# Attention, forward and backward in one stream: two constant matmuls between the score rows of three half-steps in four, the backward part two half-steps later, and the normalisation cut in two

## The chip, the cores and the metric

The kernel runs on one core of one Trainium2 chip. The metric is device time in microseconds (us) of one execution, as the median of several runs. A second execution is recorded by the profiler; its own time and the span of its instructions are given below beside the median. The engines are called PE (TensorE, the matrix unit), ACT (ScalarE), DVE (VectorE), POOL (GpSimd) and SP (SyncE, which issues the DMAs).

## What is computed

The reference mixes two branches of a layer and returns the output together with the gradients of all its weights. The branch that matters here is multi-head attention over 2048 tokens with 32 heads of width 18:

```
qkv = (x @ wqkv) -> q, k, v           # 32 heads, width 18
scores = q k^T * 18 ** -0.5
p = softmax(scores);  o = p v;  a = o @ wo
out = g * a + (1 - g) * b             # b: a state-space convolution
grads = vjp(out)(grad_out)            # of x, wqkv, wo and ten others
```

The backward pass of attention needs, for each head and each pair of token blocks, the probabilities once with keys along the partitions and once with queries along them, the product of dO with V, `ds = p * (dO V^T - delta)`, and three contractions that give dV, dQ and dK.

## The kernel before, in words

The kernel has five stages. The first projects q, k and v (up to about 240 us). The second is the attention stage, from about 240 to 2533 us; the change is in it alone. After it come the output projections and weight gradients, the convolution branch and its gradients, and a final mixing stage.

**Tiling.** Four heads form a group `g` (8 groups); each head is padded to 32 partitions, so that four heads fill 128. Queries are taken in blocks `b` of 512 (4 blocks), so there are 32 units `(g, b)`. Keys are taken in 16 tiles `i` of 128.

**The loop.** The stage is written out by hand: `manual_schedule` fixes the order of instructions on PE, ACT, DVE and POOL as the program emits them. The order on SP is left to a planner. The loop variable is a half-step `G`; 32 of them (`NST`) are a unit, 1024 in all (`NTOT`). The forward work of half-step `G` and the backward work of half-step `G2 = G - OFF` are interleaved; `OFF` is 37 before the change, so the backward stream of a unit starts when the forward stream is five half-steps into the next one. `s` below is the number of a half-step in its unit.

**One half-step.** In two rounds `x = 0, 1`, PE computes three *rows* each, a matmul of 32 partitions by 512 columns on a quarter of the array. P1 makes a block of forward scores; ACT turns it into `PT` (L592). P3 makes the same scores with queries along the partitions; ACT turns it into `eb` (L596). P2 is dO V^T; DVE multiplies it by `PT` into `ds` (L601). Rows of P1 and P3 share four PSUM banks ("S"), rows of P2 two ("dP"). So ACT has four exponentials a half-step and DVE two products.

**Bursts.** After the rows come the contractions, with 32 output partitions each so that four run side by side on quarters of the array: eight matmuls of 512 columns for dV (`dv_burst`), eight for dQ (`dq_burst`), twice eight of 256 columns for dK (`dk_half`), in this order over four half-steps that will be called phases 0 to 3 (`G2 % 4`). They share one PSUM bank, `accB`. At the end of phases 0, 1 and 3 DVE adds the bank to a sum in SBUF (`ev`: L461 `dvacc`, L478 `dqa`, L502 `dkacc`). The forward contraction `accO` has a bank of its own and four matmuls in two of the four half-steps (`G % 4` of 3 and 0). Before the change these are phases 2 and 3.

**Normalisation.** When `accO` of a unit is complete, `post_forward` copies it out on ACT (`f0`). Two half-steps later (`s` = 2) `f1` transposes it on PE into an "S" bank and has six DVE instructions (L397 to L407): the reciprocal, `Ob`, `dOa`, their product, its sum, and minus that sum as an extra column of `dOa`. Then two DMAs are issued, one storing `Ob` and (`f2`) one transposing `dOa` into `dOaT`, which the rows P2 of the backward stream read.

**Group loads.** Every four units the operands of the next group are loaded. The tiles `VaT`, `Ktok` and `Qtok` exist once, so their loads wait for the last reader of the group before.

Of the kernel before, what the change touches and what calls it, by code (L numbers as in the profile page):

```python
# [12 lines left out]
F32 = mybir.dt.float32  # L13
# [4 lines left out]
P = 128  # L18


def build(tc, aps, dbg_aps=None, stages=("s1", "attn", "post", "s4", "final")):
# [39 lines left out]
    with ExitStack() as gctx:  # L61
# [280 lines left out]
        if "attn" in stages:  # L342
            KB = 512
            NQ = S // KB
            TPQ = KB // P
            DA = HP
            with ExitStack() as ctx:
                ctx.enter_context(tc.manual_schedule(engines={mybir.EngineType.PE, mybir.EngineType.Activation, mybir.EngineType.DVE, mybir.EngineType.Pool}))
                ga = ctx.enter_context(tc.tile_pool(name="ga", bufs=2))
                ptp = ctx.enter_context(tc.tile_pool(name="ptp", bufs=20))  # L350
                work = ctx.enter_context(tc.tile_pool(name="awork", bufs=2))
                apsp = ctx.enter_context(tc.tile_pool(name="aps", bufs=1, space=bass.MemoryType.PSUM))
                ident_f = work.tile([P, P], F32, tag="ident_f", bufs=1, name="ident_f")
# [30 lines left out]
                def post_forward(g, b, acc):  # L384
                    U = UN[(g, b)]
                    st = {}

                    def f0():
                        st["oT"] = work.tile([P, KB], F32, tag="oT", name="oT")
                        nc.scalar.copy(st["oT"], acc)  # L390

                    def f1():
                        po = apsp.tile([P, TPQ, 4, HP], F32, tag="S", bufs=4, name="ps_o")
                        for qi in range(TPQ):
                            nc.tensor.transpose(po[:, qi, :, :].rearrange("p a b -> p (a b)"), st["oT"][:, qi * P:(qi + 1) * P], ident_f)
                        rl = work.tile([P, TPQ, 4], F32, tag="rl", name="rl")
                        nc.vector.reciprocal(rl, po[:, :, :, DH])  # L397
                        rlb = rl.unsqueeze(3).to_broadcast([P, TPQ, 4, DH])
                        Ob = work.tile([P, TPQ, 4, DH], BF, tag="Ob", name="Ob")
                        da = U["dOa"]  # L400
                        nc.vector.tensor_tensor(Ob, po[:, :, :, 0:DH], rlb, op=A.mult)
                        nc.vector.tensor_tensor(da[:, :, :, 0:DH], U["dO"], rlb, op=A.mult)
                        prod = work.tile([P, TPQ, 4, DH], F32, tag="prod", bufs=1, name="prod")
                        nc.vector.tensor_tensor(prod, da[:, :, :, 0:DH], Ob, op=A.mult)
                        dl = work.tile([P, TPQ, 4], F32, tag="dl", name="dl")
                        nc.vector.tensor_reduce(dl, prod, axis=AX.X, op=A.add)
                        nc.vector.tensor_scalar(da[:, :, :, DH], dl, -1.0, None, op0=A.mult)  # L407
                        nc.sync.dma_start(O_d[:, b * TPQ:(b + 1) * TPQ, 4 * g * DH:4 * (g + 1) * DH], Ob.rearrange("p t a b -> p t (a b)"))

                    def f2():  # L410
                        U["dOaT"] = work.tile([P, TPQ, P], BF, tag="dOaT", name="dOaT")
                        nc.sync.dma_start_transpose(out=U["dOaT"], in_=U["dOa"].rearrange("p t a b -> p (t a b)"))
                    return f0, f1, f2
# [18 lines left out]

                NST = 2 * NT
                NU = NG * NQ
                OFF = NST + 5
                units = [(g, b) for g in range(NG) for b in range(NQ)]
                accO = {}
                todo = {}
# [1 line left out]
                def at(n, f):  # L440
                    todo.setdefault(n, []).append(f)

                def accB(name):
                    return apsp.tile([P, KB], F32, tag="accB", name=name)

                def dv_burst(g, b, kq, half):
                    U = UN[(g, b)]
                    acc = accB("accV")
                    for n_ in range(2):
                        ii = 2 * half + n_  # L450
                        for j in range(4):
                            mm(acc[HP * j:HP * (j + 1), :], lhsT=U["dOa"][:, ii, j, :], rhs=U["eb"].pop((kq, ii, j)),
                               start=(n_ == 0), stop=(n_ == 1), tile_position=(0, HP * j))

                    def ev():
                        if b == 0 and half == 0:
                            DKV[("v", g, kq)] = work.tile([P, KB], F32, tag="dvacc", bufs=4, name="dvacc")
                            nc.vector.tensor_copy(DKV[("v", g, kq)], acc)
                        else:
                            a_ = DKV[("v", g, kq)]  # L460
                            nc.vector.tensor_tensor(a_, a_, acc, op=A.add)  # L461
                    return ev

                def dq_burst(g, b, p):
                    U = UN[(g, b)]
                    acc = accB("accQ")
                    for n_ in range(2):
                        i = 2 * p + n_
                        for j in range(4):
                            mm(acc[HP * j:HP * (j + 1), :], lhsT=grp_t[g]["Ktok"][:, i, j, :], rhs=U["ds"][i][:, j, :],  # L470
                               start=(n_ == 0), stop=(n_ == 1), tile_position=(0, HP * j))

                    def ev():
                        if p == 0:
                            U["dqa"] = work.tile([P, KB], F32, tag="dqa", name="dqa")
                            nc.vector.tensor_copy(U["dqa"], acc)
                        else:
                            nc.vector.tensor_tensor(U["dqa"], U["dqa"], acc, op=A.add)  # L478
                    return ev

                def dk_half(g, b, p, h, st):
                    U = UN[(g, b)]
                    if h == 0:
                        st["acc"] = accB("accK")
# [22 lines left out]
                for G in range(NTOT + OFF + 16):  # L507
# [13 lines left out]
                    if 0 <= G2 < NTOT:  # L521
                        u2, s2 = divmod(G2, NST)
                        r2 = (units[u2][0], units[u2][1], s2)
                    rows = []
                    for x in range(2):
                        if r1:
                            g, b, i, j0 = r1
                            T = grp_t[g]
                            rows.append(("P1", g, b, i, j0 + x, row("P1", g, b, T["KaT"][:, i * P:(i + 1) * P], T["QaT"][:, b * KB:(b + 1) * KB], j0 + x)))
# [10 lines left out]
                            j2 = 2 * par_ + (1 - x)  # L540
                            rows.append(("P2", g, b, i2, j2, row("P2", g, b, T["VaT"][:, i2 * P:(i2 + 1) * P], U["dOaT"].rearrange("p t q -> p (t q)"), j2)))
                    evs = []
                    if G % 4 == 1 and G2 >= 4:
                        p_ = (G2 - 4) // 4
                        if p_ < NTOT // 4:
                            u_, q_ = divmod(p_, NST // 4)
# [4 lines left out]
                    if G % 4 == 2 and G2 >= 5:  # L551
# [7 lines left out]
                    if G % 4 in (3, 0) and G2 >= 10:  # L559
                        p_ = (G2 - 10) // 4  # L560
                        if p_ < NTOT // 4:
                            u_, q_ = divmod(p_, NST // 4)
                            g, b = units[u_]
                            h_ = 0 if G % 4 == 3 else 1
# [7 lines left out]
                    if G % 4 in (3, 0) and G >= 3:  # L572
                        i_ = (G - 3) // 4 * 2 + (1 if G % 4 == 0 else 0)
                        u_, i_ = divmod(i_, NT)
                        if u_ < NU:
# [6 lines left out]
                            if i_ == NT - 1:  # L582
                                f0, f1, f2 = post_forward(g, b, accO.pop((g, b)))
                                evs.append(f0)
                                at(("pre", G + 2), f1)
                                at(("pre", G + 2), f2)
                    for (kind, g, b, i, j, ps) in rows:
                        U = UN[(g, b)]
                        if kind == "P1":
# [735 lines left out]
```

## Time and profile before

| what | value |
|---|---|
| median of 2 runs | 3977.11 us (3976.38 to 3977.84) |
| profiled execution, its own time | 3971.29 us |
| span of its instructions | 3969.6 us |
| mean granted PE clock | 0.624 of full speed |
| busy share of the span: PE, DVE, ACT | 77%, 74%, 73% |
| attention stage, first to last `PT` | 241.7 to 2467.5 us |
| its last part, backward work alone | 2467.5 to 2533.2 us |

The page of the profile gives busy time by engine, a strip of 40 slices (each 99 us) with the busy tenths of each engine and the PE clock in tenths, the chain of work that ended last, and the costliest groups of instructions with the idle time in front of them. A busy PE record runs from a matmul's issue to its modelled end, and matmuls overlap, so a PE that is always busy need not be at its peak. In the names of matmuls the moving operand stands first: `ps_P<-QaT_g,KaT_g` is a row P1, `ps_P<-KaT_g,QaT_g` a row P3, `ps_P<-dOaT,VaT_g` a row P2.

### The profile page before, as it was taken

What the parts mean: (1) busy time and instruction counts of PE and PEld (TensorE: products, weight loads), DVE (VectorE), ACT (ScalarE), POOL (GpSimd) and SP (SyncE); (2) the same over time, 40 slices, a digit from 0 to 9 for tenths busy, and PEclk for the clock granted to TensorE, in tenths of its full rate; (3) what the DMA queues carried; (4) which work ended last, traced back from release to release, by engine and by line L of the source; (5) the groups of instructions that cost most, each with busy time, mean ns of one, the idle gap of its engine ahead of it and who ended that gap; (6) DMA issues with size and microseconds to landing.
All of it is one profiled execution on the core that took longest, in us unless ns stands there. A gap on an engine that the chain in (4) does not pass through costs nothing. (4 is left out here: it accounts for less than half of the span.)

```text
span 3969.6 us, 64388 instructions
## 1 busy us (share of the span) xinstructions
PE 3044.3 (77%) x24050; PEld 1070.9 (27%) x24050; DVE 2943.6 (74%) x5147; ACT 2878.8 (73%) x5308; POOL 62.9 (2%) x141
## 2 busy tenths in 40 slices
PE   8979999999999999999999999598255444544411
PEld 2312222222222222222222222145133333333310
DVE  5628878878778778878778788521488888888877
ACT  4569999989989989989999998311466666666401
POOL 0000000000000000000000000100000000000000
PEclk9956656656566556666665565599565555555555
DMA  8537787887787887887887887966455655665457
GB/s 196 168 98 129 136 160 131 136 160 130 137 158 132 135 158 133 140 157 132 148 150 127 141 142 127 226 173 140 80 104 108 112 104 104 108 109 99 72 145 175
DMA packets 1858940, 538.18 MB, mean 136 GB/s; under 512 B 1771744, under 2 KB 1837354, under 8 KB 1858627
## 3 DMA queue, kind: packets, MB, share of 16 engines
q1 hardware_dynamic: 1858626, 534.07, 70.5%
q8 instruction: 189, 3.10, 0.3%
q14 instruction: 125, 1.02, 0.1%
HBM read 102.10 MB, written 60.96 MB: 41 GB/s over the span
## 5 line engine op out<-in xcount | busy, mean ns | idle before, releaser
L601 DVE TENSOR_TENSOR ds<-ps_P,PT 128x512 bf16<-128x512 f32 x2048 | 1355.2, 687 | 359.7 <-PE ps_P L30 235.5
L592 ACT ACTIVATE PT<-ps_P 128x512 bf16<-128x512 f32 x2048 | 1303.5, 641 | 146.8 <-PE ps_P L30 134.2
L596 ACT ACTIVATE eb<-ps_P 128x512 bf16<-128x512 f32 x2048 | 1318.8, 646 | 21.3 <-PE ps_P L30 21.2
L30 PE MATMUL ps_P<-dOaT,VaT_g 32*128 32x512 bf16 x2048 | 1072.5, 550 | 40.8 <-DMA VaT_g<-VaT_d 31.8
L30 PE MATMUL ps_P<-KaT_g,QaT_g 32*128 32x512 bf16 x2048 | 1030.5, 541 | 34.6 <-ACT PT L592 6.1
L30 PE MATMUL ps_P<-QaT_g,KaT_g 32*128 32x512 bf16 x2048 | 978.3, 556 | 30.0 <-DMA KaT_g<-KaT_d 6.0
L30 PEld LDWEIGHTS <-KaT_g 32*128 32x128 bf16 x2048 | 145.8, 101 | 672.5 <-issue 655.8
L30 PE MATMUL accO<-PT,Vtok_g 128*32 128x512 bf16 x2048 | 307.9, 585 | 0.0
L30 PEld LDWEIGHTS <-VaT_g 32*128 32x128 bf16 x2048 | 192.2, 96 | 409.2 <-issue 368.6
L30 PE MATMUL accK<-dsT,Qtok_g 128*32 128x256 bf16 x4096 | 293.2, 381 | 10.7 <-DMA Qtok_g<-QaT_d 5.4
L30 PE MATMUL accQ<-ds,Ktok_g 128*32 128x512 bf16 x2048 | 242.6, 568 | 1.3 <-DVE dvacc L461 0.8
L30 PE MATMUL accV<-eb,dOa 128*32 128x512 bf16 x2048 | 242.0, 567 | 0.6 <-DVE dkacc L502 0.6
L30 PEld LDWEIGHTS <-QaT_g 32*128 32x128 bf16 x2048 | 174.0, 98 | 168.5 <-issue 157.0
L30 PE MATMUL uvp<-RX,E1e 128*128 128x64 bf16 x1152 | 134.2, 290 | 106.3 <-DVE E1e L892 106.3
L30 PE MATMUL tps<-RX,T0w 128*128 128x32 bf16 x576 | 38.4, 233 | 215.2 <-DVE yd L1027 189.9
L873 ACT ACTIVATE kk<-ph,magc 128x512 f32<-128x512 f32 x144 | 91.2, 686 | 147.7 <-DVE E1e L891 112.7
L30 PE MATMUL ph<-thr,lrow 3*128 3x512 bf16 x288 | 126.7, 569 | 86.8 <-ACT ab L866 60.1
L461 DVE TENSOR_TENSOR dvacc<-dvacc,accV 128x512 f32<-128x512 f32 x224 | 153.5, 685 | 34.5 <-PE accV L30 31.0
L478 DVE TENSOR_TENSOR dqa<-dqa,accQ 128x512 f32<-128x512 f32 x224 | 153.2, 684 | 26.6 <-PE accQ L30 22.6
L30 PEld LDWEIGHTS <-E1e 128*128 128x128 bf16 x1152 | 125.3, 123 | 127.3 <-DVE E1e L892 126.7
L30 PE MATMUL ybp<-Rw,E1n 128*128 128x31 bf16 x1152 | 70.1, 233 | 103.5 <-ACT ydi L964 100.8
L878 DVE SCALAR_TENSOR_TENSOR kk<-kk,ph 128x512 f32<-128x512 f32 x144 | 95.1, 681 | 73.0 <-ACT kk L873 73.0
(273 smaller groups left out, 3374.9 us busy)
## 6 DMA issues: line engine op xcount, KB each, us to landing
T0w<-Kp_d SPq DMA_DIRECT2D x36, 512.0 KB
dsT<-ds SPq DMA_TRANSPOSE x512
dqkv_d<-dtk SPq DMA_DIRECT2D x96, 72.0 KB
dqkv_tok<-dqkv_d SPq DMA_DIRECT2D x1, 6912.0 KB
Md_d<-mst SPq DMA_DIRECT2D x144, 36.0 KB
ga_d<-ga_st SPq DMA_DIRECT2D x16, 288.0 KB
dxm_d<-dxm SPq DMA_DIRECT2D x16, 288.0 KB
skw<-Md_d SPq DMA_DIRECT2D x72, 64.0 KB
```

Of the source, the lines that this page charges most:

```text
L30: return nc.tensor.matmul(out, lhsT=lhsT, rhs=rhs, start=start, stop=stop, **kw)
L461: nc.vector.tensor_tensor(a_, a_, acc, op=A.add)
L478: nc.vector.tensor_tensor(U["dqa"], U["dqa"], acc, op=A.add)
L592: nc.scalar.activation(U["PT"][i][:, j, :], ps, ACT.Exp)
L596: nc.scalar.activation(e, ps, ACT.Exp)
L601: nc.vector.tensor_tensor(U["ds"][i][:, j, :], ps, U["PT"][i][:, j, :], op=A.mult)
L873: nc.scalar.activation(B_["kk"][h][:, 4 * q:4 * q + 4, :], ph, ACT.Identity, bias=magc, scale=1.0)
L878: nc.vector.scalar_tensor_tensor(v_, v_, MAGIC, B_["ph"].pop((h, q)), op0=A.subtract, op1=A.subtract)
```

## The change

Four edits, all in the attention stage.

1. A function `fill` issues two matmuls (`NFILL`) of 128 by 128 by 512 with the reversal matrix `J_bf` as weights and the identity, repeated four times, as moving operand. It is called between the rows of round 0 and round 1 in phases 0, 1 and 2, and writes into the `accB` bank that the burst of that half-step then takes over and starts afresh. The bank is taken at that place, and no longer in the burst.
2. `OFF` goes from 37 to 39, and the phases are counted by `G2` instead of `G`. Relative to `G2` the bursts stay where they were. The `accO` matmuls, which go by `G`, now fall in phases 0 and 1.
3. `f1` ends after `dOa`. The product, its sum, the extra column and the store of `Ob` move into `f2`, which runs one half-step later (`s` = 3) and then transposes `dOa` as before.
4. There are 21 `PT` buffers for 20, and one each of `oT` and `dqa` for two.

```
-                ptp = ctx.enter_context(tc.tile_pool(name="ptp", bufs=20))
+                NFILL = 2
+                ptp = ctx.enter_context(tc.tile_pool(name="ptp", bufs=21))
...
-                        st["oT"] = work.tile([P, KB], F32, tag="oT", name="oT")
+                        st["oT"] = work.tile([P, KB], F32, tag="oT", bufs=1, name="oT")
...
+                        st["Ob"] = Ob
                         nc.vector.tensor_tensor(Ob, po[:, :, :, 0:DH], rlb, op=A.mult)
                         nc.vector.tensor_tensor(da[:, :, :, 0:DH], U["dO"], rlb, op=A.mult)
+
+                    def f2():
+                        da, Ob = U["dOa"], st["Ob"]
                         prod = work.tile([P, TPQ, 4, DH], F32, tag="prod", bufs=1, name="prod")
...
                         nc.sync.dma_start(O_d[:, b * TPQ:(b + 1) * TPQ, 4 * g * DH:4 * (g + 1) * DH], Ob.rearrange("p t a b -> p t (a b)"))
-
-                    def f2():
                         U["dOaT"] = work.tile([P, TPQ, P], BF, tag="dOaT", name="dOaT")
...
-                OFF = NST + 5
+                OFF = NST + 7
...
+                ACC = []
+                fill_r = ident_bf.unsqueeze(1).to_broadcast([P, 4, P])
+
+                def fill(acc, n, w=4):
+                    o_ = acc[:, (4 - w) * P:4 * P].rearrange("p (a b) -> p a b", b=P)
+                    for _ in range(n):
+                        mm(o_, lhsT=J_bf, rhs=fill_r[:, 0:w, :])
...
-                    acc = accB("accV")
+                    acc = ACC.pop()
...
+                    ph = G2 % 4 if 4 <= G2 < NTOT + 4 + (0, 1, 6, 0)[G2 % 4] else None
+                    if ph == 2 and G2 < 10:
+                        ph = None
                     for x in range(2):
+                        if x == 1 and ph in (0, 1, 2):
+                            ACC.append(accB(("accV", "accQ", "accK")[ph]))
+                            fill(ACC[0], NFILL)
...
-                    if G % 4 == 1 and G2 >= 4:
+                    if G2 % 4 == 0 and G2 >= 4:
...
-                                at(("pre", G + 2), f2)
+                                at(("pre", G + 3), f2)
```

(The conditions of the dQ and dK bursts change from `G % 4` to `G2 % 4` in the same way; `dqa` becomes a single buffer as `oT` does.)

More of the change, by code (lines that the diff above doesn't have):

```diff
@@ L465, in dq_burst @@
                     U = UN[(g, b)]
-                    acc = accB("accQ")
+                    acc = ACC.pop()
                     for n_ in range(2):
@@ L474, in ev @@
                         if p == 0:
-                            U["dqa"] = work.tile([P, KB], F32, tag="dqa", name="dqa")
+                            U["dqa"] = work.tile([P, KB], F32, tag="dqa", bufs=1, name="dqa")
                             nc.vector.tensor_copy(U["dqa"], acc)
@@ L483, in dk_half @@
                     if h == 0:
-                        st["acc"] = accB("accK")
+                        st["acc"] = ACC.pop()
                     acc = st["acc"]
@@ L550, in build @@
                                 at(("pre", G + 3), lambda g=g, kq=q_ // 2: store_grad(DKV.pop(("v", g, kq)), g, 2, kq * TPQ, 1.0))
-                    if G % 4 == 2 and G2 >= 5:
+                    if G2 % 4 == 1 and G2 >= 5:
                         p_ = (G2 - 5) // 4
@@ L558, in build @@
                                 at(("pre", G + 3), lambda g=g, b=b: store_grad(UN[(g, b)].pop("dqa"), g, 0, b * TPQ, c_scale))
-                    if G % 4 in (3, 0) and G2 >= 10:
+                    if G2 % 4 in (2, 3) and G2 >= 10:
                         p_ = (G2 - 10) // 4
@@ L563, in build @@
                             g, b = units[u_]
-                            h_ = 0 if G % 4 == 3 else 1
+                            h_ = 0 if G2 % 4 == 2 else 1
                             if h_ == 0:
```

## The prediction

> **What bounds the kernel now.** First the strip of the page, for the attention stage (slices 3 to 25):
>
> ```profile
> ACT  4569999989989989989999998311466666666401
> ...
> PEclk9956656656566556666665565599565555555555
> ```
>
> ACT is busy nine tenths, and the PE clock lies between a half and full. Then the groups of the page, with the idle time before each:
>
> ```profile
> L601 DVE TENSOR_TENSOR ds<-ps_P,PT 128x512 bf16<-128x512 f32 x2048 | 1355.2, 687 | 359.7 <-PE ps_P L30 235.5
> L592 ACT ACTIVATE PT<-ps_P 128x512 bf16<-128x512 f32 x2048 | 1303.5, 641 | 146.8 <-PE ps_P L30 134.2
> L596 ACT ACTIVATE eb<-ps_P 128x512 bf16<-128x512 f32 x2048 | 1318.8, 646 | 21.3 <-PE ps_P L30 21.2
> ```
>
> ACT's idle time, 146.8 + 21.3 = 168 us, is all that a faster PE can return. In the timeline, ends of packed ACT instructions lie 0.491 us apart, so a half-step with four exponentials takes at least 1.964 us. By windows of the stage, the middle and the last part:
>
> ```profile
> 282.50:2467.50 2185.00, 2082.61 (x15864) 529.39 (x15863) 1742.73 (x2890) 2040.77 (x4064) 36.93 (x86) 0.61 0.80 141
> 2467.50:2533.20 65.70, 63.00 (x452) 12.38 (x449) 62.76 (x108) 44.09 (x82) 2.58 (x6) 0.53 0.96 164
> ```
>
> Here the fields behind the stretch are PE, PEld, DVE, ACT, POOL, clock, DMA share and GB/s. Counted by the ends of ACT's instructions, ACT loses 185 us against its packed pace: 37 at `s` = 5 (seven group loads), 61 at `s` = 1 to 3 (normalisation) and 87 spread over the rest. The waits say of the loads:
>
> ```profile
> PE ps_P L30 <- DMA VaT_g<-VaT_d: 31.8, 7, 5.5
> ```
>
> Of the 87, about 10 are waits for `Qtok`. The other 77 are lost while the clock is low. Five neighbouring windows of 3.41 us, the step in which the clock record changes:
>
> ```profile
> 2142.27:2145.68 3.41, 3.41 (x30) 0.76 (x26) 2.77 (x5) 3.17 (x7) 0.00 (x0) 0.50 1.12 121
> 2145.68:2149.09 3.41, 3.19 (x34) 1.03 (x31) 3.28 (x6) 3.41 (x9) 0.00 (x0) 1.00 0.59 111
> 2149.09:2152.51 3.42, 2.98 (x31) 0.92 (x28) 2.72 (x5) 3.42 (x9) 0.00 (x0) 1.00 0.69 127
> 2152.51:2155.92 3.41, 2.97 (x24) 0.89 (x20) 3.33 (x6) 3.41 (x9) 0.00 (x0) 1.00 0.72 132
> 2155.92:2159.33 3.41, 3.41 (x35) 1.11 (x35) 2.42 (x5) 3.37 (x8) 0.00 (x0) 0.50 0.84 159
> ```
>
> At 1.00 ACT is busy all the time (3.41 of 3.41), at 0.50 not. What moves the clock? I added up, for each such window of the stage, matmul columns times the share of the array they fill, as a share of what the granted clock allows. Of 82 cold windows from 0.72 to under 0.76, 35 were followed by a full clock, and all 29 above; of 376 below, 13. Of 76 warm windows under 0.37 the clock fell after 73, of 58 above 0.39 after none. In work that is one threshold, 0.37 to 0.39 of the full-speed array. Four half-steps hold 56 matmuls of 512 columns on a quarter (two of 256 counted as one): 7168 full columns. At ACT's pace of 7.856 us these are 0.38 of 2.4 columns per ns (a 512-column matmul on the whole array repeats every 216 ns at full clock). The kernel sits on the threshold, and 140 of 627 windows are warm.
>
> [...]
>
> **The fills and the clock.** Each fill is 2 x 512 columns on the whole array; three in four half-steps make 10240 columns. At 8.2 us a quad that is 0.52, well above the threshold. The clock should stay up and ACT's 77 us go: **-77** (0 if the clock stays as it is).
>
> **What the fills cost: a wait.** PE is in order. The fill in phases 1 and 2 waits until DVE has emptied `accB`; behind it stand the three rows of round 1, for which ACT and DVE wait. From a warm stretch, PE and then DVE:
>
> ```profile
> 2151.75 0.38 PE L30 MATMUL ps_P<-dOaT,VaT_g 32*128 32x512 bf16 x1
> 2152.07 0.62 PE L30 MATMUL accV<-eb,dOa 128*32 128x512 bf16 x8
> 2152.62 0.38 PE L30 MATMUL ps_P<-QaT_g,KaT_g 32*128 32x512 bf16 x1
> ...
> 2153.22 0.37 PE L30 MATMUL ps_P<-QaT_g,KaT_g 32*128 32x512 bf16 x1
> 2153.71 0.37 PE L30 MATMUL ps_P<-KaT_g,QaT_g 32*128 32x512 bf16 x1
> ```
>
> ```profile
> 2152.19 0.69 DVE L601 TENSOR_TENSOR ds<-ps_P,PT 128x512 bf16<-128x512 f32 x1 [0.23 <-PE ps_P L30]
> 2152.80 0.68 DVE L461 TENSOR_TENSOR dvacc<-dvacc,accV 128x512 f32<-128x512 f32 x1
> ```
>
> From the P2 row of round 1 to its `ds` 0.44; `ds` to `dvacc` 0.61; `dvacc` 0.68; release 0.05 (as from ACT's ends to the rows they free): 1.78 us, so the fill could start at 2153.53. Fill start to the next row: 0.216 + 0.311 (a 512-column matmul before a change of array tiling) = 0.527. The P1 row goes from 2153.22 to 2154.06. A row may be late by 1.964 - (0.44 row to ACT + 0.597 exponential + 0.05) = 0.87 us before ACT stalls. The loop P2 row, `ds`, `ev`, fill, P2 row takes 1.78 + 0.53 = 2.31, 0.35 more than a half-step, and it is walked twice, from phase 0 to 1 and from 1 to 2. Relative to the earliest start of its half-step's first row (P1 of round 1 at 0.98, P3 and P2 at 1.47): the fill of phase 0 waits for the short `dkacc` (0.41) until 1.01, so round 1 goes at 1.54. In phase 1 it goes at 1.88, in phase 2 at 2.20. The limit for P1 is 0.98 + 0.87 = 1.85. ACT loses 0.03 + 0.34 = 0.37 us a quad; phase 3 has no fill and recovers. 985 half-steps with both streams are 246 quads; less 32 with a normalisation and 7 with a load, 207 x 0.37 = **+77**. Bounds: 0 if the slack is larger, 143 if both loops' excess is paid in full (0.69).
>
> **Normalisation.** DVE's work does not shrink: 2.2 us, now 1.14 (L397, L401, L402 by start to start) and 1.06 a half-step later. In a warm example of before, both behind one another, P2 waited 0.66 us on `ds`. Cut in two they would fit better, but each part now also delays an `ev` on which a fill waits. Walking the same loop, `s` = 2 is phase 3: `dkacc` ends 1.0 late, the fills of `s` = 3, 4, 5 cost ACT 0.72 + 0.95 + 0.35, so 2.0 x 32 = 64 against 61: **+3**, bounds -30 and +30. `dOaT` is issued one half-step later but first read four half-steps on, where it was three; today's wait for it is 1.2 us in all. On SP the store and this transpose pass at most the half-step's other issues.
>
> **Cold windows that remain.** From the end of the fill in phase 2 to the next in phase 0 pass about 3.2 us. A window of 3.41 us lying over that gap holds 2560 columns of rows and bursts and 0.2 us of fill, 0.37: on the threshold. By position that is about 18 times (2.4 windows in 8.2 us, 0.29 us of positions). A cold quad with fills takes 3.5 + 3.5 + 2.6 + 1.9 = 11.5 us (0.427 per round, 0.11 to 0.14 per change of tiling), 3.3 more, so two cold windows (6.8 us) cost 2 us: 0 to 36, I take **+15**.
>
> **Ends and the rest.** Two more half-steps of forward alone (40.8/39 = 1.05) and of backward alone (65.7/37 = 1.78) for two of both: +2. In the last part DVE sets the pace and the 2.31 us loop adds 0.8 in each of ten quads: together **+10**. The `accO` matmuls in phases 0 and 1 (0.21 us warm) lie in the gap before the next rows and cost nothing warm. The pools: `oT` is read at `s` = 2 and rewritten 32 half-steps later; `dqa` is read a half-step before it is rewritten; 21 `PT` cover two more half-steps: 0. The group loads stay exposed: 0.
>
> Sum: -77 + 77 + 3 + 15 + 10 = +28 on 3971.3, 3999 for a profiled execution; the median lies 5.8 above it, so **4005 us**.
>
> **Rivals.** *The fill hides* (0.20): the S banks give more slack than 0.87, the 0.37 falls to 0 to 0.1, and normalisation gains up to 30: -77 + 0 to 21 - 30 to 3 + 0 to 15 + 10, 3880 to 3950. For it: PE idles 0.5 us between the rows where the fills go. Against: it is the DVE chain, not PE's room, that is late. *The gap drops the clock* (0.15), the slower side: if the threshold lies at the upper end, 0.39, windows over the 3.2 us without fill fall cold. Each costs 2 us; beyond about 34 the change loses over 2%. At one in three to one in two quads, 82 to 123 times 2 for the 15 in the sum, 4150 to 4240. *The fills do not count* (0.06): identity and reversal matrix are nearly all zeros, and the gate may see that. Then every quad is 11.5 for 8.7: +2.8 x 246 = 690, 4690. [...] The forecast, 3950 to 4100, has 0.57; 0.02 is left.
>
> Range: all lower bounds together give -77 + 0 - 30 + 0 + 2 = -105 (3872), all upper +143 - 77 + 30 + 36 + 10 = +142 (4119); with the nearer part of the second rival I take 3880 to 4140. A change of 2% (80 us) is about what tells from none: faster 0.10 (the lower part of the first rival and what is left), slower 0.28 (the other two rivals and 0.07 of the forecast), same 0.62.
>
> **What will show it.** The PE clock near 10 tenths in slices 3 to 25, and idle before `PT` (L592) no smaller than now but ended by rows that stand behind a fill; DVE's `dvacc` and `dqa` as PE's releasers. If the idle time is under 80 us, the slack was larger; if the clock stays near 6, the fills do not count or the gap decides.

## The result, and the profile after

The changed kernel takes 4039.79 us (median of 2 runs, 4037.61 to 4041.97) against 3977.11: 62.7 us more, a ratio of 1.0153 with a 95% interval of 1.0129 to 1.0178. The profiled execution took 4037.61 us with a span of 4035.9 us, 66.3 more than the span of before. The mean granted clock rose from 0.624 to 0.815. So the clock came as wanted, and the kernel became slower all the same.

First the strip of the page after (slices of 101 us; the attention stage is slices 3 to 26):

```profile
ACT  4459989989989989989899998301366666666401
...
PEclk9859999989989989999999998589555555555555
```

The clock stands mostly at nine tenths and more up to the last part of the stage, and there, in slice 26, at a half. ACT is as busy as before. The groups of the page (busy time and mean ns of one; then the idle time before, and what ended most of it):

```profile
L618 DVE TENSOR_TENSOR ds<-ps_P,PT 128x512 bf16<-128x512 f32 x2048 | 1397.6, 689 | 483.0 <-PE ps_P L30 479.7
L609 ACT ACTIVATE PT<-ps_P 128x512 bf16<-128x512 f32 x2048 | 1304.3, 641 | 146.5 <-PE ps_P L30 144.3
L613 ACT ACTIVATE eb<-ps_P 128x512 bf16<-128x512 f32 x2048 | 1321.8, 646 | 56.5 <-PE ps_P L30 56.5
...
L30 PE MATMUL accQ<-ident_bf,J_bf 128*128 128x512 bf16 x512 | 160.2, 395 | 88.8 <-DVE dvacc L472 78.0
L30 PE MATMUL accK<-ident_bf,J_bf 128*128 128x512 bf16 x512 | 156.2, 386 | 89.0 <-DVE dqa L489 78.3
```

ACT's idle time, 146.8 + 21.3 before, is 146.5 + 56.5 now: a full clock and yet 35 us more. The last two lines are the fills of phases 1 and 2. In front of each group PE stands still for 89 us, and `dvacc` and `dqa` release it, as the prediction said. By windows (PE, PEld, DVE, ACT, POOL, clock, DMA share, GB/s), the stage splits into a head with the forward stream alone, a middle with both, and a last part with the backward stream alone:

```profile
255.10:297.80 42.70, 39.47 (x156) 7.08 (x155) 2.64 (x7) 40.16 (x82) 0.00 (x0) 0.50 0.34 75
297.80:2491.20 2193.40, 1870.18 (x17302) 564.75 (x17300) 1732.14 (x2885) 2049.47 (x4056) 36.93 (x86) 0.97 0.80 140
2491.20:2597.30 106.10, 95.15 (x534) 18.75 (x533) 68.48 (x114) 49.17 (x86) 2.58 (x6) 0.55 0.62 111
```

| part, us | before | after | difference |
|---|---|---|---|
| first stage | 241.7 | 255.1 | +13.4 |
| head | 40.8 | 42.7 | +1.9 |
| middle (clock 0.61, then 0.97) | 2185.0 | 2193.4 | +8.4 |
| last part (clock 0.53, then 0.55) | 65.7 | 106.1 | +40.4 |
| all later stages | 1436.4 | 1438.6 | +2.2 |

**The first stage** runs the same instructions in both kernels. It is longer because the clock fell earlier, at 176.5 us where it was 200.1 before. Three stretches of the kernel after:

```profile
165.00:175.00 10.00, 9.27 (x42) 3.37 (x40) 3.66 (x8) 4.71 (x8) 0.00 (x0) 1.00 0.26 106
170.00:180.00 10.00, 8.11 (x38) 3.41 (x37) 1.60 (x3) 1.60 (x3) 0.00 (x0) 0.82 0.31 122
180.00:190.00 10.00, 7.96 (x29) 3.23 (x28) 0.76 (x1) 1.00 (x2) 0.00 (x0) 0.50 0.41 110
```

In the first stretch, at full clock, 42 matmuls go in 10 us, in the last, at half clock, 29. In the kernel before, the stretch from 190 to 200 us is still at 1.00. Below, the unchanged kernel is profiled once more and has 251.2 us here; over all eleven profiles of this study the stage took 241.7 to 255.1 us. With the fall between 176 and 185 us it took 250.8 to 255.1 us, with a later one 241.7 to 248.9. I count the 13.4 us as chance. What the change does to its own stage is then 40.8 + 2185.0 + 65.7 = 2291.5 us before and 2342.2 after: **+50.7 us**.

**The middle** can be read through ACT. From the ends of ACT's instructions I took what it loses against its packed pace of 0.491 us, by the place in the unit. Such sums are good to some 5 us, since the pace is a rounded figure:

| ACT's loss in the middle, us | before | after |
|---|---|---|
| half-steps that wait for `VaT` | 31.9 | 49.0 |
| half-steps that wait for `Qtok` | 9.9 | 25.4 |
| normalisation (`s` = 1 to 4 before, 1 to 6 after) | 61.2 | 47.9 |
| all other | 82.4 | 76.5 |
| sum | 185.4 | 198.9 |

The rows of the normalisation run from the copy of `accO` to the half-step before the backward stream changes its unit. After the change they so hold one ordinary fill of phase 1 and one of phase 2 in each unit.

Of "all other", before lost 82.7 us in half-steps that touch a window at half clock, and nothing (-0.5) in those at full clock. After, it is 17.2 us in 42 half-steps that touch a half clock, and 57.7 us in 729 at full clock, 0.11 in each of phase 1 and 0.23 in each of phase 2. The loss at low clock was nearly all won, and seven eighths of what was won (57.7 of 65.5 us) went to the new wait.

The places of the falls are not those of the fills. Of 21 falls of the clock in the middle 19 lie around the seven group loads, from the half-step before a group's first P2 rows to the eleventh after; one more is at the start of the middle, and one elsewhere. At the first load PE stands still, and the clock falls at 572.4 us:

```profile
572.40:575.80 3.40, 0.00 (x0) 0.00 (x0) 0.00 (x0) 1.26 (x3) 0.00 (x0) 0.50 1.01 206
```

```profile
578.79 0.60 PE L30 MATMUL ps_P<-dOaT,VaT_g 32*128 32x512 bf16 x1 [6.67 <-DMA VaT_g<-VaT_d]
```

The waits of the stage up to 2533.2 us (total, times, longest) show where the second loss comes from:

```profile
PE accK L30 <- DVE dqa L489: 75.9, 217, 0.4
PE accQ L30 <- DVE dvacc L472: 75.3, 185, 0.8
...
PE ps_P L30 <- DMA VaT_g<-VaT_d: 41.2, 7, 6.7
...
PE accK L30 <- DMA Qtok_g<-QaT_d: 24.3, 7, 4.2
```

The seven loads of `VaT` held PE for 31.8 us before, those of `Qtok` for 5.4 us. With a PE that goes faster, the last reader of the old group is done earlier, but the transfers don't come as much earlier. In the trace, SP issues the load of `Qtok` 3.3 to 5.6 us after the last read of the old one, where it was 1.0 to 2.2 us, and that of `VaT` 1.4 to 2.3 us after in six of seven loads (0.3 in the last), where it was 0.4 to 1.2. In between SP's queue has the transposes of other tiles to issue; that it is these that hold the loads back is not shown.

**The last part.** PE by its timeline, first at full clock:

```profile
2491.69 0.59 PE L30 MATMUL accQ<-ident_bf,J_bf 128*128 128x512 bf16 x2 [0.36 <-DVE dvacc L472]
2494.01 0.59 PE L30 MATMUL accK<-ident_bf,J_bf 128*128 128x512 bf16 x2 [0.32 <-DVE dqa L489]
```

The loop of P2 row, `ds`, `ev`, fill takes 2.32 us from fill to fill. Some 9 us later the clock falls. Three windows:

```profile
2494.00:2500.00 6.00, 4.61 (x43) 1.50 (x43) 5.27 (x12) 3.18 (x7) 0.00 (x0) 1.00 0.65 120
2500.00:2506.00 6.00, 4.92 (x24) 0.91 (x20) 3.95 (x7) 1.90 (x4) 0.00 (x0) 0.58 0.67 125
2506.00:2512.00 6.00, 5.66 (x38) 1.03 (x36) 3.85 (x7) 2.88 (x5) 0.00 (x0) 0.50 0.79 96
```

It falls at 2500.93, in the normalisation of the last unit. The 3.41 us before hold array work (columns times the share of the array, as in the prediction) of 0.33 of what the full-speed array can do. The clock then stays at 0.50 to the end of the part. From then on PE and the chain of DVE go like this:

```profile
2520.18 1.01 PE L30 MATMUL accV<-ident_bf,J_bf 128*128 128x512 bf16 x2 [0.34 <-DVE dkacc L513]
...
2523.55 1.01 PE L30 MATMUL accQ<-ident_bf,J_bf 128*128 128x512 bf16 x2 [0.31 <-DVE dvacc L472]
...
2526.95 1.01 PE L30 MATMUL accK<-ident_bf,J_bf 128*128 128x512 bf16 x2 [0.33 <-DVE dqa L487]
...
2531.32 1.01 PE L30 MATMUL accV<-ident_bf,J_bf 128*128 128x512 bf16 x2 [0.35 <-DVE dkacc L513]
```

At half clock the loop takes 3.4 us, and four half-steps take 11.14 us (2531.32 less 2520.18) where they took 7.1 before (65.7 over 37 half-steps, times 4). PE is busy 5.66 of 6.00 us, but each fill waits its third of a microsecond for DVE, and the work per window stays at 0.53 to 0.67 of what the half clock allows. In the middle, the 22 windows at half clock that were followed by a full one held about 0.76 and more, the 21 that were not about 0.6 at most.

### The profile page after: what moved, and what is told of

The parts are those of the page before. It is cut to its first block, busy times and chain, and to the rows that moved or that the text cites. A ratio compares the mean times of both kernels' runs of the same rounds, so it can differ in the third digit from the quotient of the medians.

```text
span 4035.9 us, 67215 instructions
## 1 busy us (share of the span) xinstructions
PE 2876.8 (71%) x25586; PEld 1112.6 (28%) x25586; DVE 2939.5 (73%) x5147; ACT 2894.1 (72%) x5308; POOL 63.0 (2%) x141
## 5 line engine op out<-in xcount | busy, mean ns | idle before, releaser
L609 ACT ACTIVATE PT<-ps_P 128x512 bf16<-128x512 f32 x2048 | 1304.3, 641 | 146.5 <-PE ps_P L30 144.3
L613 ACT ACTIVATE eb<-ps_P 128x512 bf16<-128x512 f32 x2048 | 1321.8, 646 | 56.5 <-PE ps_P L30 56.5
L30 PE MATMUL ps_P<-dOaT,VaT_g 32*128 32x512 bf16 x2048 | 814.9, 400 | 42.1 <-DMA VaT_g<-VaT_d 41.2
L30 PE MATMUL ps_P<-KaT_g,QaT_g 32*128 32x512 bf16 x2048 | 801.0, 396 | 34.4 <-ACT PT L609 6.6
L30 PE MATMUL ps_P<-QaT_g,KaT_g 32*128 32x512 bf16 x2048 | 792.9, 398 | 24.9 <-ACT PT L609 11.5
L30 PEld LDWEIGHTS <-J_bf 128*128 128x128 bf16 x1600 | 150.5, 97 | 507.1 <-issue 420.6
L30 PE MATMUL accK<-dsT,Qtok_g 128*32 128x256 bf16 x4096 | 213.2, 287 | 24.3 <-DMA Qtok_g<-QaT_d 24.3
L30 PE MATMUL accQ<-ident_bf,J_bf 128*128 128x512 bf16 x512 | 160.2, 395 | 88.8 <-DVE dvacc L472 78.0
L30 PE MATMUL accK<-ident_bf,J_bf 128*128 128x512 bf16 x512 | 156.2, 386 | 89.0 <-DVE dqa L489 78.3
L30 PE MATMUL accO<-PT,Vtok_g 128*32 128x512 bf16 x2048 | 211.8, 399 | 0.0
L30 PE MATMUL accV<-ident_bf,J_bf 128*128 128x512 bf16 x512 | 163.0, 401 | 43.4 <-DVE dkacc L513 12.5
L30 PE MATMUL tps<-RX,T0w 128*128 128x32 bf16 x576 | 38.4, 233 | 215.2 <-DVE yd L1044 201.8
L30 PE MATMUL accQ<-ds,Ktok_g 128*32 128x512 bf16 x2048 | 162.4, 395 | 0.0
```

The source lines that it names most:

```text
L30: return nc.tensor.matmul(out, lhsT=lhsT, rhs=rhs, start=start, stop=stop, **kw)
L609: nc.scalar.activation(U["PT"][i][:, j, :], ps, ACT.Exp)
L613: nc.scalar.activation(e, ps, ACT.Exp)
```

## The experiments

All kernels compute the whole function; the results of the fills are always overwritten. This table has every one with its median, its ratio to the kernel before on the same chip, and from its profile the length and clock of middle and last part and how often the clock fell from full to half in the middle.

| kernel | median us | ratio (95% interval) | middle, clock | last part | falls |
|---|---|---|---|---|---|
| before, second profile | 3974.82 | | 2181.6, 0.63 | 64.5 | 85 |
| no fills in the last part | 3996.12 | 1.0056 (1.0039 to 1.0074) | 2191.5, 0.96 | 67.2 | 25 |
| no fills at all | 4023.74 | 1.0117 (1.0088 to 1.0146) | 2223.6, 0.69 | 68.9 | 172 |
| fills in an "S" bank | 3976.57 | 1.0009 (0.9994 to 1.0024) | 2169.8, 0.91 | 68.7 | 91 |
| fills alone, in `accB` | 4060.14 | 1.0223 (1.0195 to 1.0251) | 2229.8, 0.94 | 100.9 | 25 |
| S bank, phases 2 and 3 | 3922.72 | 0.985 (0.9819 to 0.988) | 2120.6, 0.92 | 67.0 | 70 |
| no fills, `accO` moved back | 4020.25 | 1.0099 (1.0079 to 1.0119) | 2218.5, 0.62 | 70.2 | 79 |
| before + one fill in every half-step | 3896.90 | 0.9782 (0.9756 to 0.9808) | 2104.5, 0.95 | 64.5 | 22 |
| the same, two buffers for `VaT` | 3867.63 | 0.9712 (0.9696 to 0.9728) | 2075.2, 0.97 | 64.3 | 17 |

The changed kernel itself has 21 falls, the kernel before 77.

### The first four: the last part, the fills, their bank, the other edits

My theory after the result: the fills in the last part cost 40 us at half clock, the wait on DVE gives back most of the gain of the clock in the middle, and the other edits cost little. Each kernel takes one of these away.

**No fills in the last part.** The changed kernel with this line in place of the call:

```
-                            fill(ACC[0], NFILL)
+                            fill(ACC[0], NFILL if G < NTOT else 0)
```

> The changed kernel without its fills in the last part of the attention stage (G of 1024 and more, backward work alone); the fills of the middle stay. In the changed kernel this part took 106.1 us where it had taken 65.7. Theory: the fills themselves cost this, because without P1 rows and accO the array's work stays under the clock's threshold, so each fill runs at half clock and each waits for DVE; then the last part falls to 66 to 72 us and the whole to about 4002. Rival: two more half-steps, the moved accO and the later normalisation lengthen it, fills or not; then it stays above 90 us and the whole above 4025.

The last part by its window:

```profile
2478.60:2545.80 67.20, 63.08 (x476) 12.68 (x473) 65.78 (x114) 45.80 (x86) 2.58 (x6) 0.58 0.99 168
```

106.1 us become 67.2. The fills of the last ten quads cost 38.9 us, with the clock at about a half either way: 0.55 there, 0.58 here. The middle is unchanged, 2191.5 for 2193.4 us.

**No fills at all.** `NFILL = 0`, so that the later backward stream, `accO` in phases 0 and 1 and the divided normalisation are left.

> The changed kernel with no fill at all (NFILL 0); the backward stream two half-steps later, the accO matmuls in phases 0 and 1 and the cut normalisation stay. Theory: the clock goes back to about 0.6 in the middle part, the 80 us lost behind the fills go and some 77 us lost at low clock return, the last part is 69 us; the whole is 3970 to 3990. Rival: what the changed kernel lost came from the other edits (accO beside the long bursts, the normalisation in two pieces); then the whole stays above 4010. The first stage, 255.1 us in the changed kernel for 241.7 before with the same instructions, is 13 us shorter again if its length is chance, and stays if it is of the change.

This missed my figure: 4023.74 us. The theory had it that these edits cost little. Its middle, and `PT` among its groups:

```profile
296.00:2519.60 2223.60, 2081.14 (x15830) 516.71 (x15828) 1764.72 (x2884) 2028.03 (x4056) 36.93 (x86) 0.69 0.80 138
```

```profile
L609 ACT ACTIVATE PT<-ps_P 128x512 bf16<-128x512 f32 x2048 | 1325.2, 652 | 198.1 <-PE ps_P L30 195.2
```

ACT waits 198.1 us before `PT`, 146.8 in the kernel before, although the clock is a little higher. By place, ACT loses 18.2 us in the normalisation, 43 less than before, and 168.5 us in "all other", 86 more. That lies in phases 0 and 1 alone: 0.52 to 0.60 us in a half-step of phase 0 and 0.22 to 0.41 in one of phase 1, none in phases 2 and 3. In phases 0 and 1 the four matmuls of `accO` now stand beside the long bursts of dV and dQ; a run below takes them away from there.

**Fills in an "S" bank.** The same fills at the same place, but written into the bank of the P1 row of round 1, which that row then overwrites. They wait for ACT like the row itself, and no longer for DVE. There are none in the last part, where no P1 row exists.

```
-                            fill(ACC[0], NFILL)
...
-                def row(kind, g, b, l, r, j):
+                def row(kind, g, b, l, r, j, nf=0):
...
+                    if nf:
+                        fill(ps, nf)
                     mm(ps, lhsT=l[r0:r0 + DA], rhs=r[r0:r0 + DA], tile_position=(r0, 0))
...
+                                                                nf=NFILL if x == 1 and ph in (0, 1, 2) else 0)))
```

> The changed kernel with the same fills at the same place, but written into the PSUM bank that the P1 row of round 1 overwrites next, so that they wait for ACT (as that row does anyway) and not for DVE to empty accB. There is no P1 row in the last part, so no fill there either. Theory of the prediction (each fill in phases 1 and 2 waits for DVE, 0.37 us a quad): the clock stays near 0.97, the 80 us lost outside normalisation and loads fall to under 20, the last part to about 70; the whole is about 3930. Rival: the fills cost PE's own time, or their change of array tiling delays the rows, whatever bank they write; then the 80 us stay and only the last part is won: 4000.

3976.57 us, which is neither. Half of the theory stands: at full clock ACT loses nothing any more in the steady half-steps (-3.6 us for 57.7 with the fills in `accB`), so the wait on DVE was the whole of that loss. But the clock falls 91 times in the middle, for 21 with the fills in `accB`, and half-steps that touch a low clock lose 82.7 us. Two windows of the same width as the steps of the clock:

```profile
952.07:955.49 3.42, 3.10 (x30) 1.02 (x30) 2.85 (x6) 3.42 (x9) 0.00 (x0) 1.00 0.84 158
955.49:958.90 3.41, 3.41 (x21) 0.64 (x21) 1.94 (x3) 2.44 (x6) 0.00 (x0) 0.50 0.82 154
```

and the fills in PE's timeline around the first:

```profile
951.70 0.38 PE L30 MATMUL ps_P<-ident_bf,J_bf 128*128 128x512 bf16 x1
...
955.40 0.53 PE L30 MATMUL ps_P<-ident_bf,J_bf 128*128 128x512 bf16 x1
```

ACT is busy all of 952.07 to 955.49 and PE 3.10 us of it, yet no fill lies inside: the fills stand at 951.70 and 955.40. The work of that window is 0.32, and the next is at half clock. This is the gap from phase 2 over phase 3 to phase 0. Measured from fill to fill, at full clock, it is 3.70 us here (median of 193) and 3.38 us in the changed kernel (of 236). There the wait on DVE pushes the fill of phase 2 back and so shortens the gap. Its thin windows hold 0.36 to 0.40 of work: there are 58, and 3 were followed by a fall. In the S-bank kernel 80 windows hold 0.30 to 0.38, and 63 were. That the shorter gap keeps the clock up is read from these windows; no run changed the gap alone.

**Fills alone, in `accB`.** The kernel before plus `fill` as in the change, with the old `OFF`, the old normalisation and the old buffers.

```
+                        if x == 1 and ph in (0, 1, 2):
+                            ACC.append(accB(("accV", "accQ", "accK")[ph]))
+                            fill(ACC[0], NFILL)
```

> The kernel before with the fills of the change alone: the backward stream stays at 37 half-steps, the normalisation in one piece, the accO matmuls in phases 2 and 3. Theory: the fills make the change's loss, so this comes out near the changed kernel, the normalisation a little worse (+16 us, the gain that the cut showed): 4030 to 4060, clock near 0.97 in the middle part. Rival: the other edits are needed for the fills or make the loss themselves: under 4000 or over 4080.

```profile
2519.50:2620.40 100.90, 90.60 (x506) 17.64 (x503) 65.13 (x109) 46.68 (x82) 2.56 (x6) 0.54 0.64 112
```

The last part is 100.9 us long with the old order too, so it is the fills that make it so. At full clock the steady half-steps lose 65.4 us, of them 0.05 in phase 1 and 0.30 in phase 2: the same 0.35 a quad with the other order of `accO`. The whole is 2.23% slower than before, where all four edits are 1.53% slower. So beside the fills the other edits gain something, while by themselves they cost 1.17%.

### The next four: where to put the fill

**S bank, phases 2 and 3.** If the gap of the S-bank kernel is what drops its clock, fills in the two half-steps with the short bursts should do better.

```
-                                                                nf=NFILL if x == 1 and ph in (0, 1, 2) else 0)))
+                                                                nf=NFILL if x == 1 and ph in (2, 3) else 0)))
```

> As e3 (fills in the bank of the P1 row of round 1), but the fills stand in phases 2 and 3 instead of 0, 1 and 2, two each. In e3 the ScalarE lost nothing in half-steps at full clock (-3.6 us in 547) and 79 us in the 219 that touched a window of half clock. Theory: that was the gap, since phases 2 and 3 have less work (accO stands in 0 and 1) and one window of 3.41 us fits between the fill of phase 2 and that of phase 0; with fills in 2 and 3 each half-step has 2304 full columns, 0.49 of the array at ScalarE's pace, and no window falls under 0.39. Then the clock of the middle part is 0.96 or more, its steady losses fall from 79 to under 20, and the whole is 3900 to 3925. Rival: the low windows come from the loads and the unit starts and last because the clock is slow to return; then the clock stays near 0.91 and the whole near 3975.

```profile
286.10:2406.70 2120.60, 1952.42 (x16812) 554.41 (x16810) 1733.39 (x2885) 2010.83 (x4056) 36.73 (x86) 0.92 0.84 145
```

3922.72 us, as expected, with fewer fills than the changed kernel. The reason given was only half right: the clock was to stay at 0.96 and is 0.92. It falls 70 times, now nearly always in phase 0 or 1 (68 of 70), where no fill stands. The gap has moved with the fills.

**No fills, `accO` moved back.** This is to test whether the place of `accO` is what the kernel without fills loses by. `accO` goes two half-steps later, into phases 2 and 3 as before, and `f1`, `f2` keep their half-steps, one half-step nearer to the copy than they were.

```
-                    if G % 4 in (3, 0) and G >= 3:
-                        i_ = (G - 3) // 4 * 2 + (1 if G % 4 == 0 else 0)
+                    if G % 4 in (1, 2) and G >= 5:
+                        i_ = (G - 5) // 4 * 2 + (1 if G % 4 == 2 else 0)
...
-                                at(("pre", G + 2), f1)
-                                at(("pre", G + 3), f2)
+                                at(("pre", G + 1), f1)
+                                at(("pre", G + 2), f2)
```

> As e2 (no fills, backward stream 39 half-steps behind, normalisation cut in two), but the accO matmuls come two half-steps later, so that they stand in phases 2 and 3 again as in the kernel before; f1 and f2 follow one and two half-steps after the copy. In e2 the middle part took 2223.6 us for 2185.0 before, with 168 us lost outside loads and normalisation for 82, nearly all of it behind phases 0 and 1. Theory: this is the accO beside the long bursts: PE at half clock has 2304 columns there and 1280 in phases 2 and 3, where before it had 1792 in each. Then the loss falls back to 70 to 95 and the middle part to 2125 to 2150 (the normalisation keeps its gain of some 40), the whole to 3925 to 3950. Rival: the later backward stream or the cut itself costs; then the middle part stays above 2200.

The time, 4020.25 us, missed the 3925 to 3950. By place the answer is split. "All other" falls from 168.5 to 80.0 us, as low as in the kernel before: the place of `accO` was worth those 88 us. But the normalisation rises from 18.2 to 98.5 us, 54 of it at `s` = 2, since `f1` stands in front of PE one half-step after the copy: PE waits for the copy 30 times, 34.3 us in all. Whether the divided normalisation with `accO` in phases 2 and 3 can be had at 18 us isn't settled by this run.

**Before, with one fill in every half-step, in the S bank.** No gap, no wait on DVE, `accO` and everything else as before.

```
+                NFILL = 1
...
-                def row(kind, g, b, l, r, j):
+                def row(kind, g, b, l, r, j, nf=0):
...
+                    if nf:
+                        fill(ps, nf)
                     mm(ps, lhsT=l[r0:r0 + DA], rhs=r[r0:r0 + DA], tile_position=(r0, 0))
...
+                                                                nf=NFILL if x == 1 and G2 >= 4 else 0)))
```

> The kernel before (backward stream 37 half-steps behind, accO in phases 2 and 3, normalisation in one piece, all pools as they were) with one fill matmul in every half-step that has both streams, in the PSUM bank of the P1 row of round 1. Theory (what helps is a clock held up without a wait on DVE and without a gap): the clock of the middle part is 0.96 or more, steady losses fall from 82 to under 15, loads rise from 42 to 60 or 75 as in all kernels at full clock, normalisation falls from 61 to 40 or 50, and the last part, without fills, stays near 66; the whole is 3905 to 3930. Rival: one matmul of 512 columns a half-step (0.49 of the array) is too little against the fluctuation; then the clock is under 0.85 and the whole above 3950.

```profile
291.60:2396.10 2104.50, 1925.75 (x16847) 629.62 (x16846) 1748.72 (x2891) 2009.68 (x4065) 36.73 (x86) 0.95 0.84 146
```

3896.90 us, 2.2% faster than before. The 777 steady half-steps at full clock together lose nothing (-4.9 us), and only 56 touch a low clock. "All other" costs 17.1 us for 82.4. This is what fills can have here without the other three edits.

**The kernel before once more**, for the first stage and the spread of the parts.

> The kernel before once more, for a second profile of its first stage, whose instructions are the same in all kernels of this study: 241.7 us in the profile of before, 255.1, 244.4, 253.3, 253.4 and 248.9 in the changed kernel and e1 to e4. If its length is chance, this one lies anywhere from 240 to 256; if the change lengthens it, it lies at 240 to 243 again.

The first stage takes 251.2 us here and 241.7 in the first profile, with the same code; middle and last part, 2181.6 and 64.5 us, agree with 2185.0 and 65.7 to 0.2% and 1.2 us.

### The last: the loads that are now exposed

In the kernel with one fill a half-step, PE's longest waits are for the group loads:

```profile
PE ps_P L30 <- DMA VaT_g<-VaT_d: 37.3, 7, 6.5
...
PE accK L30 <- DMA Qtok_g<-QaT_d: 19.5, 7, 4.6
```

A second buffer for `VaT` lets its load go early; `oT` and `dqa` give up one each for the room.

```
-                    for nm, src, nb in (("QaT", QaT_d[g], 2), ("KaT", KaT_d[g], 2), ("VaT", VaT_d[g], 1)):
+                    for nm, src, nb in (("QaT", QaT_d[g], 2), ("KaT", KaT_d[g], 2), ("VaT", VaT_d[g], 2)):
```

> e9 (the kernel before with one fill per half-step in the bank of the P1 row) with two buffers of VaT in place of one; the room comes from single buffers of oT and dqa, as in the change. In every kernel the first P2 row of a group waits for the load of VaT, 4 to 8 us seven times, since the load waits for the last reader; in the changed kernel loads cost ScalarE 74 us for 42 before. Theory: the load is a transfer of its own length behind SP's queue, so a second buffer takes VaT's wait (40 us in e9) off and leaves Qtok's (21): the middle part falls from 2104 to 2060 to 2075, the whole to 3850 to 3870. Rival: the queue on SP is the limit, and the wait moves to Qtok or Ktok, whose loads follow in the same queue; then Qtok's loss grows by what VaT's falls and the whole stays above 3885.

```profile
293.70:2368.90 2075.20, 1913.64 (x16847) 632.09 (x16847) 1743.11 (x2891) 2006.95 (x4065) 37.10 (x86) 0.97 0.85 148
```

```profile
PE accK L30 <- DMA Qtok_g<-QaT_d: 37.0, 7, 6.5
```

3867.63 us, 2.9% faster than before and the fastest version here. The loss at `VaT` went from 40.1 to 0.2 us, but nearly half of it came back behind it: that at `Qtok`, the next load that PE waits for, went from 20.9 to 38.4. Theory and rival each had about half.

## Why the prediction was right and wrong

The kernel became slower, inside the range, but by 62.7 us and not by 28. By the terms of the sum:

| term | predicted | measured |
|---|---|---|
| clock, fill's wait and remaining cold windows, together | -77 + 77 + 15 = +15 | 76.5 - 82.4 = -6 |
| normalisation | +3 | 47.9 - 61.2 = -13 |
| group loads | 0 | 74.4 - 41.8 = +33 |
| ends | +10 | 1.9 + 40.4 - 3.9 = +38 |
| sum | +28 | +52 (by the parts: +50.7) |
| first and later stages | 0 | +15.6 |

(The 3.9 are the two half-steps of 1.964 us that the middle has fewer. The 1.05 us a half-step of the prediction's ends divides the head's 40.8 us by 39; the head of before has 37 half-steps, so it is 1.10, which moves the sum by 0.1 us.)

**Right: what bounds, and the clock.** At a clock of 0.97 the 82.7 us at low clock became 17.2, where the sum left 15. The prediction's edge, 0.37 to 0.39, held at full clock: of some 3500 windows with work of 0.40 or more, in eleven profiles, none was followed by a fall, and of 205 under 0.37 in the kernel without fills 169 were. At half clock the kernel before shows no sharp edge, 35 rises after 82 windows from 0.72 to under 0.76, by the prediction's count; in the middle after the change all 22 came after about 0.76 and more. That the 17.2 is so near the 15 is luck, though. The prediction laid these windows on the gap between fills, about 18 times by position; 19 of the 21 falls lie at the group loads, which it had put at nothing. PE's busy time alone did not go with the clock here: in the row of 2506.00 above PE is busy 5.66 of 6.00 us and the clock stays at 0.50, and in the prediction's row of 2152.51 PE is busy 2.97 of 3.41 us at 1.00 and the next window is at 0.50. The clock records of the kernel before and of the changed one hold 0.50 and 1.00 alone.

**Right: the fill's wait.** Predicted were 0.03 us in phase 1 and 0.34 in phase 2, 0.37 a quad; measured are 0.11 and 0.23, together 0.34. The loop of 2.31 us is 2.32. The total is 57.7 us for 77, because fewer half-steps are both steady and at full clock (729, or 182 quads, for 207). The S-bank kernel takes the wait away and the loss with it, so its cause is shown.

**Wrong: "In the last part DVE sets the pace and the 2.31 us loop adds 0.8 in each of ten quads".** Together with the group loads below, this is the step that failed: it stood for 8 of the +10 of the ends, and that term measured +38. It priced the last part at full clock, though its clock before was 0.53, in a row that the prediction itself showed, and though the same text had the tool for it, the work of a window: the loop of 3.4 us, with two fills in it, left every window at 0.53 to 0.67 of what the half clock allows, and after none of them did the clock rise. Once one window was thin, at 0.33, each fill's wait kept the next windows thin; this is read from the rows above. Without the fills in that part, 38.9 us come back. I didn't separate by a run how much of it is the half clock and how much the wait; by the loop at full clock it would have been about 8.

**Wrong: "The group loads stay exposed: 0".** This term stood at nothing without a reason, and it is the largest miss of the sum: the loads cost ACT 41.8 us before and 74.4 after, 33 more. All kernels with a high clock lose more at `VaT` than before (38 to 50 us for 32), except the one with two buffers. At `Qtok` a high clock alone doesn't do it. In the S-bank kernel with fills in phases 2 and 3, at a clock of 0.92, SP issues this load 0.0 to 2.3 us after the last reader, and PE hardly waits:

```profile
PE accK L30 <- DMA Qtok_g<-QaT_d: 6.9, 4, 2.1
```

So what delays the loads in the change stays open. The run with the second buffer shows only that nearly half of what one load no longer waits for is waited for at the next.

**Wrong in size: normalisation.** +3 was a sum of two effects, and both are larger: without fills, dividing it (with the new place of `accO`) is worth 43 us, 18.2 for 61.2, and in the S-bank kernel it stays at 17.4; the fills in `accB`, which wait for the delayed `ev`, take 30 of it back. Some 11 of these 30 are the ordinary wait of the fills in phases 1 and 2, 0.34 us in each of 32 units.

**Right only under the full clock: "accO ... cost nothing warm".** At full clock there is no loss in phase 0: the 57.7 us lie in phases 1 and 2. At the clock that the kernel has without fills, 0.69, `accO` behind the long bursts costs 86 us. So the change needs its fills, and the sum was right not to charge it.

**The rivals.** "The fill hides" didn't come in the change, but the S-bank kernel is that rival without its wait, and it met the other one: "The gap drops the clock" is what happened there, 91 falls. In the change itself the windows over the gap hold 0.36 to 0.40, and 3 of 58 were followed by a fall; the gap is 3.38 us there for 3.70, with the wait that costs 57.7 us. "The fills do not count" is refuted: with identity and reversal matrix the clock of the middle is 0.97, without them 0.69.

**Chance.** 13.4 us of the profiled difference lie in the first stage. What sets the moment at which the clock falls there was not tested.

## What to carry to other kernels

Before adding matmuls to keep the clock up, add up the array work of each window of 3.41 us and see which windows lie under the level at which the clock fell (here it fell after none of 0.40 or more); then put a little filling into every stretch rather than much into some. One matmul in each half-step, in the bank of the next row, won 2.2%. Two in three half-steps of four, with the change's other edits, left the time as it was in that bank (1.0009) and lost 1.5% in the bank that waits for DVE, 38.9 us of it in the last part. Let the filler wait only for what the next instruction on PE waits for anyway, and leave it out of stretches whose work stays low with the filler's own waits: in the last part here the windows stayed at 0.53 to 0.67 of what the half clock allows, and two fills took 1.01 us for 0.59 at full clock. Then look at what the faster engine uncovers, here the group loads, which cost 74.4 us for 41.8.

## What the runs showed of the hardware that was not expected

- In the last part of the changed kernel the clock fell once, at 2500.93, and stayed at 0.50: the loop that waits for DVE grew from 2.32 to 3.4 us, and the work per window stayed at 0.53 to 0.67 of what the half clock allows, where the rises in the middle came after about 0.76 and more.
- With the wait that delays the fill, the stretch without fills is 3.38 us long for 3.70 in the S-bank kernel, and the clock falls 21 times in the middle for 91. No run changed that stretch alone.
- The fills' operands are nearly all zeros, and the clock of the middle is 0.97 with them for 0.69 without. Added up by columns and share of the array like any other matmul, they leave the falls at the same work: of some 520 windows at full clock with 0.40 or more in the middle of the changed kernel none was followed by a fall, and none of some 50 in the kernel before.
